# Exchanging the pads of the tile pools: moving blocks of the feed-forward products at 64 instead of 192 bytes mod 256

## The chip, the cores and the metric

The kernel runs on one core of one Trainium2 chip. The metric is the device time of one execution in microseconds (us): 850.94 us before the change, the median of three runs (850.67 to 851.38).

## The reference

Sigmoid attention is followed by two feed-forward stages: a maximum over three products, and then a PReLU stage with a hidden width of 2048. Cut to what matters:

```python
scores = scale * np.matmul(q, k.transpose(0, 1, 3, 2)) - np.log(S)   # 4 x 12 heads, 448 x 64
attn = 1.0 / (1.0 + np.exp(-scores))
x = np.matmul(attn, v)                                               # -> 1792 x 768
h = np.maximum(np.maximum(x @ w1, x @ w2), x @ w3)                   # 768 wide
y = h @ w_out
h = y @ w_in                                                         # 2048 wide
g = np.maximum(h, 0.0) + alpha * np.minimum(h, 0.0)
out = g @ w_out2                                                     # 1792 x 768
```

All arrays are float32.

## The kernel before

**Two parts.** `attention` does scores and the weighted sum of values in 64 by 64 tiles of TensorE, four of them side by side (lines 563 and 584). After it, `ff` and `ff3` do all the feed-forward products. Each product is computed by a scheme with seven block products in place of eight (numbered 0 to 6), and each float32 factor is split into a high and a low float32r part, of which three of the four partial products are kept: low weight by high input, high weight by low input, and high by high. Every partial product is a matmul with a stationary block of 128 x 128 (the weight part) and a moving block of 128 x 448 (the input part); all 3528 of them are issued by `group` at line 694, and each one has its own load of the stationary block. They stand in long runs that add up in one PSUM bank: nine in a run for the products with three blocks of depth (tiles `u_0X`, `u_1W` and so on) and more in the last product (`eX`, `eW`, `eV`).

**What the other engines do meanwhile.** ScalarE and VectorE unpack weights from 64-bit words, form sums and differences of blocks, split them into high and low parts, and move results out of PSUM. A list of pending operations with credits per engine (`op`, `advance`, `need`) decides which of them is put into the program after which product; it counts columns, and addresses do not enter into it.

**Where tiles lie.** Weight tiles (`wslot`, 384 columns of 4 bytes, that is 6 x 256 bytes) come from pools that begin at a multiple of 256 bytes in each partition. Input tiles (`slot`, 448 columns, 7 x 256 bytes) come from pool `a` on the left, and from pools `c` and then `e` on the right, which grow towards lower addresses. A small tile named `pad` is taken once from each pool. In pool `a` it is taken ahead of the slots, so the slots begin that much higher; in the right pools it is taken behind them, and since the pool ends at a fixed address, its slots begin that much lower. In the last product, pool `l` holds weight parts (`lf`) first, then a pad, then the input parts (`rf`). In the built program every one of the 3528 matmuls of line 694 has its stationary block at 0 mod 256 and its moving block at 192 mod 256. In the attention, both operands of every matmul lie at 0 mod 256, before and after the change.

Of the kernel before, what the change touches and what calls it, by code (L numbers as in the profile page):

```python
# [15 lines left out]

P = 128
SCRATCH = 4096
HEADS, BATCH, SEQ, WIDTH, FF2 = 12, 4, 448, 768, 2048
HK = WIDTH // P // 2  # L20
NU, KP = 3 * HK, FF2 // P // 2
# [41 lines left out]
def kernel(  # L63
# [33 lines left out]
    def pad(pool, w):  # L97

        if pool not in padded:
            padded.add(pool)  # L100
            pools[pool].tile([P, w], F32, tag="pad", name=f"pad_{pool}")

    def slot(nm, pool="a", w=TW, dt=F32):
        if pool == "a":
            pad(pool, 48)
        t = pools[pool].tile([P, w], dt, tag="s" + pool, name=nm, bufs=room[pool])
        if pool != "a":
            pad(pool, 16)
        return t

    def wslot(nm, dt=F32, pool="w"):

        if pool != "w":
            return slot(nm, pool, HF, dt)
        return wpool.tile([P, HF], dt, tag="ws", name=nm, bufs=21)
# [91 lines left out]
    def need_ops(*ops):  # L207

        chain = [o for o in ops if o.step is None]
        for o in chain:  # L210
            chain += [d for d in o.deps if d.step is None and d not in chain]
        while any(o.step is None for o in ops):
            now[0] += 1
            n = len(urgent) + len(flow)
            for todo in (urgent, flow):
                for o in [o for o in todo if o in chain]:
                    if ready(o, False) and (o.gate is None or o.gate()):
                        emit(o)
                        todo.remove(o)
            if len(urgent) + len(flow) == n:  # L220
                advance(0, free=True)
            assert now[0] < 99999
# [4 lines left out]
    def drain():  # L227
        while urgent or flow:
            n = len(urgent) + len(flow)
            advance(0, free=True)  # L230
            assert len(urgent) + len(flow) < n or now[0] < 9999
# [182 lines left out]
    def forms(q, of, into, homes, soon=False):  # L414
# [10 lines left out]
        def cut(c, x, *deps):  # L425
            def make(y):
                if y == "h":
                    home[c] = homes(c, 2)
                    take(home[c], 2)
                    if into is hf:  # L430
                        hhome[g, c, r] = home[c]
                return slot(f"{q}_{c}{y}", home[c], TW, F32R)

            o = split_ops(
                into[g, c, r], make, lambda: b[x][0], TW, *deps, gate=lambda: homes(c, 2), soon=soon
            )
            if (c, x) not in ((2, "T"), (1, "21")):
                o.after.append(lambda: used(x))
            return o

        def t1():
            p = homes(None, 1)
            take(p)
            b["T"] = slot(f"{q}_t", p), p
            tensor_op(b["T"][0], b["12"][0], b["11"][0], ALU.subtract)
            used("11")
# [610 lines left out]
    def ff3(ps_m, dpool, fd, wd, slopes, seq, turn_left):  # L1057
# [6 lines left out]
        def tile_l(tag, nm, w, bufs, dt=F32):  # L1064
            return pools["l"].tile([P, w], dt, tag=tag, name=nm, bufs=bufs)
# [144 lines left out]
        def plan():  # L1210
            for n in range(1, 14):
                if n % 2 == 0:
                    for kp in range(KP):
                        left_ops(n // 2, kp)
                for kp in range(KP):
                    right_ops(n, kp)
# [86 lines left out]
        def run(stored):  # L1303
            plan()
            for k in range(7):
                for g, mp in order:
                    if (k, g, mp) == (0, 0, 1):
                        need_ops(*stored, *firsts)
                        turn_left()

                        lf[1, 0]["h"] = tile_l("lf", "lf1_0h", HF, 2 * KP, F32R)
                        pad("l", 48)
                        for x in (2, 3):
                            kept[x, order[0]] = tile_l(f"p{x}", f"p{x}_00", TW, 2 * HK)
                    e_group(k, g, mp)
            drain()
# [3 lines left out]
    with tc.manual_schedule():  # L1320
# [22 lines left out]
        def turn_left():  # L1343
            left.close()
            pools["l"] = ctx.enter_context(
                tc.tile_pool(name="slots_l", bufs=1, reuse_waits="tile")
            )
            del pools["a"]
# [64 lines left out]
```

## Time and profile before

| | before |
|---|---|
| median of 3 runs | 850.94 us (850.67 to 851.38) |
| the profiled execution's own time | 851.17 us |
| its span, first to last instruction | 849.3 us |
| TensorE matmuls busy (PE) | 844.4 us, 99% |
| TensorE weight loads busy (PEld) | 732.8 us, 86% |
| VectorE (DVE) | 655.4 us, 77% |
| ScalarE (ACT) | 517.7 us, 61% |
| GpSimd (POOL) | 146.9 us, 17% |

Busy time is the time in which at least one instruction of the engine ran. Matmuls overlap: the end of one lies past the start of the next, so how fast TensorE goes is read from the time between starts, or from the length of a run in the chain, and not from the duration of one matmul.

### The profile page before, as it was taken

How to read it: one execution, taken by the hardware profiler on the slowest of the kernel's cores; microseconds unless marked ns; L12 is line 12 of the kernel's file. 1: busy time of each engine (PE TensorE's matmuls, PEld its weight loads, DVE VectorE, ACT ScalarE, POOL GpSimd, SP SyncE). 2: the span in 40 equal slices, each digit the busy share in tenths (PEclk: the TensorE clock that was granted, in tenths of full speed). 3: DMA queues.
4: the chain of work that ended last, by engine and by line, in shares of the span. 5: the costliest groups of instructions: out<-in, count | busy, mean ns of one | idle time of the engine just before them, and what ended most of it. 6: DMA issues, size and time to landing. Idle time of an engine off the chain costs nothing.

```text
span 849.3 us, 14230 instructions
## 1 busy us (share of the span) xinstructions
PE 844.4 (99%) x4878; PEld 732.8 (86%) x4878; DVE 655.4 (77%) x1304; ACT 517.7 (61%) x1006; POOL 146.9 (17%) x272
## 2 busy tenths in 40 slices
PE   9999999999999999999999999999999999999998
PEld 4444678999999999999999999999999999999997
DVE  1889888789979988797488988977768687868631
ACT  6888997644655464656377867776657554453530
POOL 1464000003200312410001322221211010001110
PEclk9999999999999999999999999999999999999999
DMA  7899632445845765987531766534547999437111
GB/s 269 277 371 350 214 110 87 131 135 191 284 155 159 240 207 171 360 314 222 157 95 65 243 196 232 184 131 155 172 162 265 328 351 371 144 118 242 69 44 54
DMA packets 77863, 170.45 MB, mean 201 GB/s; under 512 B 11120, under 2 KB 51856, under 8 KB 77792
## 3 DMA queue, kind: packets, MB, share of 16 engines
q1 hardware_dynamic: 60048, 106.38, 39.7%
q0 software_dynamic: 17456, 62.83, 19.6%
q8 instruction: 38, 0.62, 0.3%
q10 hardware_dynamic: 288, 0.34, 0.1%
q14 instruction: 33, 0.27, 0.1%
HBM read 123.12 MB, written 46.40 MB: 200 GB/s over the span
## 4 chain that ended last, share of the span: by engine, by line
PE 99%; DVE 0%; ACT 0%; issue 0%
PE u_0X L694 17%; PE u_1X L694 17%; PE eW L694 10%; PE eX L694 10%; PE u_1W L694 9%; PE u_0W L694 9%; PE sc L563 8%; PE pav L584 7%; PE u_0V L694 4%; PE u_1V L694 4%; PE eV L694 3%; PE warm L629 0%; DVE o L1232 0%; ACT o L1230 0%; DVE zeros L625 0%
## 5 line engine op out<-in xcount | busy, mean ns | idle before, releaser
L571 ACT ACTIVATE a<-sc,bias_s 128x896 f32<-128x896 f32 x84 | 83.2, 1010 | 12.7 <-PE sc L563 11.6
L563 PE MATMUL sc<-qt,kt 64*64 64x448 f32 x672 | 83.1, 540 | 0.0
L584 PE MATMUL pav<-a,vt 64*64 64x448 f32 x672 | 82.0, 536 | 0.0
L281 DVE CUSTOM_DVE_ANT_0 wt<-wr,wt 128x768 uint16<-128x768 uint16 x112 | 62.6, 559 | 3.9
L273 DVE SCALAR_TENSOR_TENSOR wr<-wr 128x384 uint32<-128x384 uint32 x112 | 62.0, 554 | 0.4
L265 ACT ACTIVATE wr<-wr 128x384 uint32<-128x384 uint32 x112 | 62.1, 554 | 0.0
L563 PEld LDWEIGHTS sc<-qt,kt 64*64 64x64 f32 x672 | 36.3, 134 | 29.3 <-issue 14.8
L584 PEld LDWEIGHTS pav<-a,vt 64*64 64x64 f32 x672 | 35.9, 133 | 28.1 <-issue 19.1
L262 ACT ACTIVATE wt<-wr 128x384 f32<-128x384 f32 x92 | 51.0, 554 | 14.7 <-DMA wr<-in_weights_dram 11.6
L741 DVE SCALAR_TENSOR_TENSOR r<-n,nalpha,r 128x448 f32<-128x448 f32 x64 | 42.8, 682 | 14.5 <-ACT n L738 14.4
L774 POOL DMA_DIRECT2D gd<-r x48 | 25.9, 541 | 159.6 <-DVE r L741 145.2
L245 POOL DMA_DIRECT2D wd<-wt x32 | 17.7, 553 | 174.4 <-DVE wt L281 173.6
L889 ACT COPY u<-u_1X 128x448 f32<-128x448 f32 x40 | 21.3, 533 | 38.5 <-PE u_1X L694 38.4
L272 DVE TENSOR_SCALAR wt<-wt 128x384 uint32<-128x384 uint32 x112 | 39.8, 355 | 5.5 <-ACT wt L262 4.8
L889 ACT COPY u<-u_0X 128x448 f32<-128x448 f32 x40 | 21.3, 533 | 35.6 <-PE u_0X L694 35.5
L874 ACT COPY u_0V<-u_0X 128x448 f32<-128x448 f32 x20 | 10.3, 518 | 48.0 <-PE u_0X L694 48.0
L311 DVE TENSOR_TENSOR u<-u_1W,u 128x448 f32<-128x448 f32 x34 | 21.2, 623 | 23.8 <-ACT u L889 19.5
L311 DVE TENSOR_TENSOR u<-u_0W,u 128x448 f32<-128x448 f32 x34 | 21.2, 623 | 18.3 <-ACT u L889 14.4
L1287 ACT COPY p<-eW 128x448 f32<-128x448 f32 x12 | 6.4, 534 | 34.1 <-PE eW L694 34.1
L599 DVE COPY x<-pav 128x448 f32<-128x448 f32 x12 | 7.5, 624 | 22.3 <-PE pav L584 22.3
L737 ACT ACTIVATE r<-u 128x448 f32<-128x448 f32 x32 | 18.5, 579 | 5.6 <-DVE u L311 5.6
L311 DVE TENSOR_TENSOR p<-eX,p 128x448 f32<-128x448 f32 x12 | 7.5, 623 | 16.4 <-PE eX L694 16.4
(821 smaller groups left out, 2791.7 us busy)
## 6 DMA issues: line engine op xcount, KB each, us to landing
wr<-in_weights_dram SPq DMA_DIRECT2D x100, 384.0 KB, 3.6
gl<-gd SPq DMA_DIRECT2D x79, 224.0 KB, 4.4
wl<-wd SPq DMA_DIRECT2D x64, 192.0 KB, 4.5
gd<-r POOLq DMA_DIRECT2D x48, 224.0 KB, 2.7
gl_T<-gdT SPq DMA_DIRECT2D x32, 224.0 KB, 5.1
hr<-hd POOLq DMA_DIRECT2D x28, 224.0 KB, 5.9
wd<-wt POOLq DMA_DIRECT2D x32, 192.0 KB, 3.8
kt<-in_k_dram SPq DMA_DIRECT2D x23, 224.0 KB, 5.3
```

The source lines that it names most:

```text
L262: nc.scalar.activation(st["T"].bitcast(F32), st["r"][:, :, 1].bitcast(F32), AF.Abs, scale=2.0**-112)
L265: nc.scalar.activation(st["r"][:, :, 0], st["r"][:, :, 0], AF.Copy, scale=2.0**-29)
L272: nc.vector.tensor_scalar(st["T"], st["T"], 3, None, ALU.logical_shift_left)
L273: nc.vector.scalar_tensor_tensor(out=st["r"][:, :, 0], in0=st["r"][:, :, 1], scalar=0x80000000, in1=st["r"][:, :, 0], op0=ALU.bitwise_and, ...
L281: nc.vector.tensor_tensor(out=st["T"], in0=st["r"][:, :, 0], in1=st["T"], op=ALU.add)
L311: nc.vector.tensor_tensor(out=out, in0=a, in1=b, op=op)
L563: nc.tensor.matmul(sc[g * KH : (g + 1) * KH, j, :S], keys[u, z][r, m * KH : (m + 1) * KH], queries[u, z][r], start=True, stop=True,)
L571: nc.scalar.activation(a, sc[:, :, :S], AF.Sigmoid, bias=bias_s, scale=scale)
L584: nc.tensor.matmul(pv[key][j * D : (j + 1) * D, :S], vts[u][r, m, j], a[r, j], start=start, stop=stop,)
L694: nc.tensor.matmul(ps[:, : rh.shape[-1]], lt, rh, start=(start and z == 0), stop=(stop and z == len(mms) - 1), skip_group_check=True,)
L741: nc.vector.scalar_tensor_tensor(out=s["r"], in0=s["n"], scalar=nalpha[:, f : f + 1], in1=s["r"], op0=ALU.mult, op1=ALU.add,)
L889: nc.scalar.copy(side[u, g, k], banks[X][:, :TW])
```

## The change

The two pad sizes change places: 16 columns (64 bytes) stand ahead of the slots in pools `a` and `l` where there were 48 (192 bytes), and 48 columns behind those in the right pools where there were 16.

```diff
+PAD = 16
...
     def slot(nm, pool="a", w=TW, dt=F32):
         if pool == "a":
-            pad(pool, 48)
+            pad(pool, PAD)
         t = pools[pool].tile([P, w], dt, tag="s" + pool, name=nm, bufs=room[pool])
         if pool != "a":
-            pad(pool, 16)
+            pad(pool, 64 - PAD)
         return t
...
                         lf[1, 0]["h"] = tile_l("lf", "lf1_0h", HF, 2 * KP, F32R)
-                        pad("l", 48)
+                        pad("l", PAD)
```

In the built program the moving block of all 3528 matmuls of line 694 begins at 64 mod 256 instead of 192; their stationary blocks stay at 0. The same tiles are also read and written by ScalarE, VectorE and DMAs, at 64 instead of 192. No instruction and no wait is added, removed or put elsewhere on any engine or queue: each engine's sequence, waits included, is the same but for the numbers of source lines.

## Rows read from the trace of the kernel before

**Rows 1.** The page, busy time (us, share of the span) and instructions of each engine.

```profile
PE 844.4 (99%) x4878; PEld 732.8 (86%) x4878; DVE 655.4 (77%) x1304; ACT 517.7 (61%) x1006; POOL 146.9 (17%) x272
```

**Rows 2.** Cores: span and mean granted TensorE clock.

```profile
core 0: 849.3 us, clock 0.999
```

**Rows 3.** The page, the chain that ended last, by engine and by line.

```profile
PE 99%; DVE 0%; ACT 0%; issue 0%
PE u_0X L694 17%; PE u_1X L694 17%; PE eW L694 10%; PE eX L694 10%; PE u_1W L694 9%; PE u_0W L694 9%; PE sc L563 8%; PE pav L584 7%; PE u_0V L694 4%; PE u_1V L694 4%; PE eV L694 3%; PE warm L629 0%; DVE o L1232 0%; ACT o L1230 0%; DVE zeros L625 0%
```

**Rows 4.** Waits of PE: who for whom, us in total, times, longest.

```profile
PE warm L629 <- DVE zeros L625: 1.2, 1, 1.2
```

**Rows 5.** Windows: attention, feed-forward products, tail; each engine's busy us (instructions), clock, DMA.

```profile
core 0: us, PE busy (x) PEld busy (x) DVE busy (x) ACT busy (x) POOL busy (x), PEclk, DMA share, GB/s
3.97:131.98 128.01, 128.01 (x1345) 70.79 (x1345) 100.42 (x220) 111.47 (x149) 35.69 (x65) 1.00 0.75 264
131.98:845.60 713.62, 713.62 (x3529) 661.21 (x3528) 554.24 (x1081) 404.44 (x854) 108.30 (x199) 1.00 0.57 190
845.60:849.30 3.70, 0.02 (x1) 0.00 (x0) 0.39 (x1) 0.35 (x1) 0.00 (x0) 0.84 0.19 62
```

**Rows 6.** The chain in order of time, feed-forward: start us, us, what.

```profile
201.34 1.82 PE u_0X L694 x9
203.16 1.82 PE u_1X L694 x9
```

**Rows 7.** Timeline of PE and PEld in the feed-forward: start us, us, what.

```profile
193.29 0.37 PE L694 MATMUL u_1W<-x_2h,f_2l 128*128 128x448 f32 x1
193.30 0.19 PEld L694 LDWEIGHTS u_1W<-x_2l,f_2h 128*128 128x128 f32 x1
193.50 0.36 PE L694 MATMUL u_1W<-x_2l,f_2h 128*128 128x448 f32 x1
193.50 0.19 PEld L694 LDWEIGHTS u_1W<-x_2h,f_2h 128*128 128x128 f32 x1
193.70 0.36 PE L694 MATMUL u_1W<-x_2h,f_2h 128*128 128x448 f32 x1
193.70 0.19 PEld L694 LDWEIGHTS u_0X<-x_3h,f_3l 128*128 128x128 f32 x1
193.90 0.37 PE L694 MATMUL u_0X<-x_3h,f_3l 128*128 128x448 f32 x1
```

**Rows 8.** Line 694: duration ns min/median/max, first and last start us, form.

```profile
L694 PEld LDWEIGHTS u_0W<-x_2h,f_2l x27: 187/187/188, 133.6 to 340.5; 128*128 128x128 f32 x27
L694 PE MATMUL u_0W<-x_2h,f_2l x27: 363/367/368, 133.8 to 340.7; 128*128 128x448 f32 x27
L694 PE MATMUL u_0W<-x_2l,f_2h x27: 361/361/368, 134.0 to 340.9; 128*128 128x448 f32 x27
L694 PE MATMUL u_0W<-x_2h,f_2h x27: 361/363/363, 134.7 to 341.1; 128*128 128x448 f32 x27
```

**Rows 9.** Line 563, weight loads of the attention, columns as in rows 8.

```profile
L563 PEld LDWEIGHTS sc<-qt,kt x672: 129/133/228, 3.9 to 128.8; 64*64 64x64 f32 x168
```

**Rows 10.** The chain in order of time, attention, columns as in rows 6.

```profile
59.74 0.75 PE sc L563 x8
60.49 0.75 PE pav L584 x8
...
66.50 0.75 PE pav L584 x8
67.26 0.74 PE sc L563 x7
```

**Rows 11.** Groups by line: busy us, mean ns of one, idle us before it and releaser.

```profile
L311 DVE TENSOR_TENSOR wt<-wt,wt 128x384 f32<-128x384 f32 x36 | 19.8, 551 | 0.2
L311 DVE TENSOR_TENSOR gl_T<-gl,gl_T 128x448 f32<-128x448 f32 x32 | 18.2, 620 | 0.0
```

**Rows 12.** The page, DMA issues: count, KB each, median us to landing.

```profile
gl<-gd SPq DMA_DIRECT2D x79, 224.0 KB, 4.4
wl<-wd SPq DMA_DIRECT2D x64, 192.0 KB, 4.5
```

## Prediction

> **What bounds the kernel now.** I read the busy time of the engines first: matmuls cover 99% of the span [rows 1], at a granted clock of 0.999, that is the 2.4 GHz level [rows 2]. Next the chain that ended last: it is PE for 99%, nearly all of that line 694 [rows 3]. Then PE's waits: a single one, 1.2 us, before the first matmul of all [rows 4]. So nothing that another engine or a DMA does holds TensorE up; the time is the number of matmuls times the time from one to the next. By stage, the attention takes 128.0 us, the feed-forward products 713.6 us and the tail 3.7 us [rows 5]. The profiled execution took 851.17 us with a span of 849.3, so 1.9 us lie around the span; it stands 0.23 us above the median of 850.94. The sum below is made against 851.17.
>
> The change touches the 713.6 us alone. There the window holds 3529 matmuls (one of them the attention's last), so 713.62 / 3529 = 202.2 ns from one to the next, and the chain says the same: nine in 1.82 us [rows 5, 6]. It is the same in every run of nine, whichever tiles are used.
>
> What fills these 202.2 ns? A block has 448 columns; at one column a tick of 2.4 GHz they need 186.7 ns (an estimate). The attention gives a check. From 59.74 to 67.26 us it does 80 matmuls in 7.52 us, 376 ns for the four that run side by side, against 2 x 186.7 = 373.3 ns for two passes over the columns: 2.7 ns over the stream [rows 10]. A feed-forward matmul takes 202.2, some 15 ns over its stream. The weight load explains most of that. The timeline shows each load starting within 0.01 us of the matmul ahead of it, and the next matmul starting some 0.20 us after that [rows 7]. The load lasts 187 to 188 ns [rows 8]. So load, hand-over, matmul start, next load is a closed chain, about 187.5 plus 15 ns, and the stream of the moving block is inside it, with about 202.2 - 186.7 - 2.7 = 13 ns to spare.
>
> The steps are not equal. Starts in the timeline are 0.20 or 0.21 us apart [rows 7], and the three matmuls of a triple have median durations of 367, 361 and 363 ns [rows 8]. The reader is to see a pattern of three with about 6.5 ns between the long and the short ones. With two short steps and a long one in 606.6 ns, the short one is (606.6 - 6.5) / 3 = 200.0 ns and the long one 206.5 ns. Something costs 6.5 ns in one step of three, and it is not a wait for another engine. A read of the moving block that meets the load in the same part of the memory would do that; no row proves it.
>
> **The change part by part.** It removes, adds and moves no instruction, so each term is a number of accesses at a new place times what that place adds.
>
> The attention: 0 ns, as its operands stay where they are.
>
> VectorE, ScalarE and DMAs on blocks that move from 192 to 64: taken as nothing. A VectorE sum of 384 columns at 0 mod 256 takes 551 ns, one of 448 columns at 192 takes 620 [rows 11], 1.43 and 1.38 ns a column, so no cost of the place shows. A transfer of 224 KB into blocks at 192 lands in 4.4 us, one of 192 KB into blocks at 0 in 4.5 [rows 12]. The cover is large: VectorE is busy 554 of 713.6 us and ScalarE 404 [rows 5], and PE waits for neither. Even 5% more on VectorE, 28 us, would fit in the 159 us that it is free, as long as it is spread out.
>
> The 3528 matmuls: here everything is decided, one ns on each is 3.5 us. The trace of before has only one place of the moving block against the stationary one in these products (192 against 0), so the cost is bounded from both sides. The nearest bounds are the two kinds of step that are there already. If every step is the short one, (200.0 - 202.2) x 3528 = -7.7 us, 843.4. If every step is the long one, (206.5 - 202.2) x 3528 = +15.3 us, 866.4. The far bound below is the stream alone, 186.7 + 2.7 = 189.4 ns, -45 us or 806; I leave it out of the range, since it needs a load that is no longer in the chain, and the loads last 187 ns wherever one looks. Above there is no such far row.
>
> Which value? The two streams can be followed by an estimate. The moving block's 1792 bytes pass in 186.7 ns, 9.6 bytes a ns. A load of 64 columns takes 133 ns [rows 9], one of 128 takes 187.5, so 64 columns cost 54 ns, a column 0.85 ns, and the weights are read at 4.7 bytes a ns for 108 ns. Both begin together [rows 7]. If the memory repeats every 256 bytes, which I assume and no row shows, a block at 192 is 64 bytes behind the weights' 0 and gains 4.9 bytes a ns: it meets the load at 13 ns and at 65 ns, and would meet it a third time at 118, when the load is over. A block at 64 is 192 behind and meets it at 39 and 91 ns. Two meetings either way; but the second now falls in the last 17 ns of the load. A load delayed there passes all of it on to the next matmul, while after a meeting at 13 ns the two are still settling. So I take the long step as the more frequent one after the change: two of three, (200.0 + 2 x 206.5) / 3 = 204.3 ns, +2.15 x 3528 = +7.6 us. The sum: 851.17 + 0 + 0 + 7.6 = 858.8 us.
>
> The Trainium skill speaks against any effect: TensorE: Matmul & The Clock Gate, in "Step-by-step: what each phase is for", says that TensorE reads SBUF through two independent ports, one for the moving operand and one for weights, so that loading the next weights takes no bandwidth from a running matmul. By it the third term is 0 and the sum 851.2. The even 187 to 188 ns of the loads agree with it; the pattern of three steps is not explained by it.
>
> **The rivals.**
>
> The place makes no difference (no change). Two meetings before and two after may cost the same; or the memory repeats every 128 bytes or less, and then 64 and 192, which are 128 apart, are the same place. For it: loads are equally long in 3528 cases [rows 8], and a rate of 0.85 ns a column fits the attention's loads, where both operands are at 0, and those of the feed-forward with 192 against 0 [rows 8, 9]; and the moving stream has 13 ns to spare, which hides a delay of its own. Against it: the step of 206.5 ns that comes and goes without any wait. Time: 851.2, from 850 to 852.
>
> The long step goes away (faster). If what costs 6.5 ns is the early meeting at 13 ns, when load and matmul have both just begun, a block at 64 has none before 39 ns, and all steps are short: 851.17 - 7.7 = 843.4. For it: the short step is what two of three matmuls take already. It decides from half a ns per matmul (1.7 us). Against it: with the other meeting still at 91 ns, there is no reason that the step stays short. VectorE is not in the way, 554 us of work in then 706.
>
> Every step becomes long: 866.4, the far end of the forecast's own case. For it: an even meeting in each load. Against it: the pattern of three shows that the delay shifts the next meeting.
>
> That the change does not do what it says is excluded, since the built program has all 3528 blocks at 64.
>
> **How the numbers follow.** Slower, 0.42: mostly 853 to 867, a tenth of the case beyond. No change, 0.30: 850 to 852. Faster, 0.28: from 849 down to 842 in most of it, and by less likely ways further down. The forecast is that of the likeliest, 858.8. Its own range is 853 to 867. From 842 to 867 lie about 0.36 + 0.30 + 0.20 = 0.86; I keep these ends, since both bounds of the unknown cost are inside them by little. About 0.2% (1.7 us) is what a measurement of this kernel can tell from no change; with it the chances are 0.28 faster, 0.30 same, 0.42 slower.
>
> **What the profile after would show.** If I am right, runs of nine in the chain take 1.84 us and not 1.82, the window of the products grows to about 721 us with PE still at 100% of it and no wait of PE, the attention stays at 128.0 us, and the medians of the three kinds of matmul show 367 twice. With all steps long, nine take 1.86 us; with all short, 1.80; if the place is without effect, 1.82 and the same three medians. Loads that last longer than 188 ns would show that it is the load that is delayed; loads of 187 with longer steps, that it is the hand-over or the stream. The prediction is wrong if the long step becomes rarer or disappears, if the meeting of two reads costs nothing, or if a wait of PE for VectorE appears, which would mean that the other engines feel the place after all.

## The result, and the profile after

The changed kernel takes 843.57 us (median of 6 runs, 842.73 to 844.59), the kernel before 850.99 us in the same comparison: a ratio of 0.991 with a 95% interval of 0.9897 to 0.9923. It is 7.4 us faster. Medians, ratios and intervals leave out executions over 1.5% above a kernel's shortest; in this document these are three of the ten of the kernel with both kinds of block at 0 (866.43 to 867.58 us, at a granted clock of 0.999 to 1.0 as in the other seven, and without a trace). The forecast was 858.8 us and slower; what came is, to 0.2 us, the number of the second rival (843.4, "the long step goes away").

The page of the kernel after: the span, and below it busy time, share and instructions of each engine, to be held against [rows 1].

```profile
span 840.9 us, 14230 instructions
PE 835.9 (99%) x4878; PEld 724.5 (86%) x4878; DVE 654.8 (78%) x1304; ACT 517.2 (62%) x1006; POOL 146.8 (17%) x272
```

Against [rows 1] PE lost 8.5 us of busy time; VectorE and ScalarE lost 0.6 and 0.5. PE still waits once only:

```profile
PE warm L630 <- DVE zeros L626: 1.2, 1, 1.2
```

The windows of the kernel after by stage, the products from their start at 131.31 us to their end at 837.15 [rows 5]:

```profile
core 0: us, PE busy (x) PEld busy (x) DVE busy (x) ACT busy (x) POOL busy (x), PEclk, DMA share, GB/s
3.96:131.31 127.35, 127.35 (x1346) 62.56 (x1345) 100.39 (x220) 111.46 (x149) 35.66 (x65) 1.00 0.76 266
131.31:837.15 705.84, 705.83 (x3529) 661.18 (x3528) 553.68 (x1081) 403.87 (x854) 108.30 (x199) 1.00 0.58 192
```

The products went from 713.6 to 705.8 us, 7.8 us less over 3529 matmuls, 2.2 ns on each. The span fell by 8.4 us; the other 0.66 us is an attention of 127.35 and not 128.01 us. Its blocks did not move, and in the kernels measured below the products start from 0.6 us earlier to 1.2 us later than before (counted from the first matmul) without regard to the places, so I count this as scatter.

The chain in order of time, as in [rows 6], shows the gain in each run of nine: 1.80 and not 1.82 us.

```profile
199.92 1.80 PE u_0X L695 x9
201.72 1.80 PE u_1X L695 x9
203.52 1.80 PE u_0W L695 x9
```

Line 695 (694 before), duration ns min/median/max, to be read beside [rows 8]: the loads last as long as before, and where the three medians were 367, 361 and 363 they are now 360, 362 and 363, without a long one.

```profile
L695 PEld LDWEIGHTS u_0W<-x_2h,f_2l x27: 187/187/188, 133.0 to 337.6; 128*128 128x128 f32 x27
L695 PE MATMUL u_0W<-x_2h,f_2l x27: 360/360/363, 133.2 to 337.8; 128*128 128x448 f32 x27
L695 PE MATMUL u_0W<-x_2l,f_2h x27: 360/362/363, 133.4 to 338.0; 128*128 128x448 f32 x27
L695 PE MATMUL u_0W<-x_2h,f_2h x27: 362/363/363, 134.0 to 338.2; 128*128 128x448 f32 x27
```

The start times in the trace give the step itself, the time from one matmul of this line to the next. Its mean is the time from the first to the last start, divided by 3527: 713.34 us / 3527 = 202.25 ns before, 705.53 / 3527 = 200.04 ns after. Before, the steps repeat 199, 201, 207; after, 198, 201, 201.

VectorE and the transfers, as in [rows 11, 12], did not notice the new place:

```profile
L312 DVE TENSOR_TENSOR wt<-wt,wt 128x384 f32<-128x384 f32 x36 | 19.8, 550 | 0.2
L312 DVE TENSOR_TENSOR gl_T<-gl,gl_T 128x448 f32<-128x448 f32 x32 | 18.2, 616 | 0.0
...
gl<-gd SPq DMA_DIRECT2D x79, 224.0 KB, 4.3
wl<-wd SPq DMA_DIRECT2D x64, 192.0 KB, 4.5
```

### The profile page after: what moved, and what is told of

It reads as the page before. It is cut to its first block, busy times and chain, and to the rows that moved or that the text cites. A ratio compares the mean times of both kernels' runs of the same rounds, so it can differ in the third digit from the quotient of the medians.

```text
span 840.9 us, 14230 instructions
## 1 busy us (share of the span) xinstructions
PE 835.9 (99%) x4878; PEld 724.5 (86%) x4878; DVE 654.8 (78%) x1304; ACT 517.2 (62%) x1006; POOL 146.8 (17%) x272
## 4 chain that ended last, share of the span: by engine, by line
PE 99%; DVE 0%; ACT 0%; issue 0%
PE u_0X L695 17%; PE u_1X L695 17%; PE eW L695 10%; PE eX L695 10%; PE u_0W L695 9%; PE u_1W L695 9%; PE sc L564 8%; PE pav L585 8%; PE u_0V L695 4%; PE u_1V L695 4%; PE eV L695 3%; PE warm L630 0%; DVE o L1233 0%; ACT o L1231 0%; DVE zeros L626 0%
## 5 line engine op out<-in xcount | busy, mean ns | idle before, releaser
L564 PE MATMUL sc<-qt,kt 64*64 64x448 f32 x672 | 79.4, 540 | 0.0
L585 PE MATMUL pav<-a,vt 64*64 64x448 f32 x672 | 78.7, 536 | 0.0
L263 ACT ACTIVATE wt<-wr 128x384 f32<-128x384 f32 x92 | 50.8, 553 | 14.9 <-DMA wr<-in_weights_dram 11.7
L564 PEld LDWEIGHTS sc<-qt,kt 64*64 64x64 f32 x672 | 31.5, 134 | 32.7 <-issue 19.9
L585 PEld LDWEIGHTS pav<-a,vt 64*64 64x64 f32 x672 | 31.1, 133 | 32.2 <-issue 27.9
L312 DVE TENSOR_TENSOR wt<-wt,wt 128x384 f32<-128x384 f32 x36 | 19.8, 550 | 0.2
```

The lines of the kernel that those rows point to most:

```text
L263: nc.scalar.activation(st["T"].bitcast(F32), st["r"][:, :, 1].bitcast(F32), AF.Abs, scale=2.0**-112)
L312: nc.vector.tensor_tensor(out=out, in0=a, in1=b, op=op)
L564: nc.tensor.matmul(sc[g * KH : (g + 1) * KH, j, :S], keys[u, z][r, m * KH : (m + 1) * KH], queries[u, z][r], start=True, stop=True,)
L585: nc.tensor.matmul(pv[key][j * D : (j + 1) * D, :S], vts[u][r, m, j], a[r, j], start=start, stop=stop,)
```

## The experiments

The theories: the difference between the places of the moving and the stationary block decides (DIFFERENCE), or the moving block's own place (OWN PLACE), or other engines (OTHERS); and, for what a step is made of, a chain of loads (CHAIN), stops where the two streams meet (MEETING), or a fixed cost when the weights change (HAND-OVER). In the diffs, STAT and MOVE are the places of the stationary and the moving blocks mod 256, lines left out are marked by three dots, and the lines taken out are those of the changed kernel. A mean step is the time from the first to the last start of a kernel's 3528 products, divided by 3527, unless the text says otherwise. "The kernel before" measured beside the runs was at 851.2 to 851.8 us.

### Only the difference of the places counts

Both kinds of block moved, with a wider tile ahead of the weights' pool:

```diff
+STAT, MOVE = 128, 64
...
-            pad(pool, PAD)
+            pad(pool, (MOVE - STAT) % 256 // 4)
...
-            pad(pool, 64 - PAD)
+            pad(pool, -MOVE % 256 // 4)
...
-    bias_s = const.tile([P, 32], F32, name="bias_s")[:, :1]
+    bias_s = const.tile([P, 32 + STAT // 4], F32, name="bias_s")[:, :1]
...
-                        pad("l", PAD)
+                        pad("l", (MOVE - STAT) % 256 // 4)
```

Stationary at 128, moving at 64:

> Stationary blocks at 128 and moving blocks at 64 mod 256, so the moving block lies 192 ahead of the stationary one as in the kernel before, while it begins where it does in the changed kernel. If only the difference of the two places counts (theory DIFFERENCE, the picture of two streams that meet): steps of 199, 201 and 207 ns, mean 202.2, and about 851 us. If the moving block's own place counts (rival OWN PLACE): mean step 200.0 and about 843.5 us. If the gain came from VectorE, ScalarE or DMAs at the new place (rival OTHERS): 843.5 us as well, since their blocks stay at 64.

Measured: 850.96 us, ratio 0.9995 (0.9986 to 1.0005), mean step 202.25 ns. The gain is gone though the moving blocks, which VectorE, ScalarE and the DMAs use too, lie where they do in the changed kernel. PE waits once only, 1.2 us, here as there. OWN PLACE and OTHERS fall. The chain of this kernel:

```profile
299.85 1.82 PE u_0X L695 x9
301.67 1.82 PE u_1X L695 x9
```

The mirror image, stationary at 128 and moving at 192 (`STAT, MOVE = 128, 192`):

> Moving blocks at 192 as in the kernel before, stationary ones at 128, so the moving block lies 64 ahead of the stationary one as in the changed kernel. DIFFERENCE: steps of 198 and 201 ns, mean 200.0, and 843.5 us, though the moving block begins where it did before and VectorE, ScalarE and DMAs find their blocks at 192. Any theory by which 64 itself is the better place: 851 us.

Measured: 843.73 us, ratio 0.9905 (0.9888 to 0.9921), mean step 200.03 ns. The moving blocks lie where they did before the change, and the whole gain is there. Its chain:

```profile
300.17 1.80 PE u_1X L695 x9
301.96 1.80 PE u_0X L695 x9
```

So DIFFERENCE holds for these two: 64 ahead is the fast pair and 192 ahead the slow one, at both places of the stationary blocks that were tried. Since 64 minus 128 does the same as 192 minus 0, and 64 and 192 differ, the pattern repeats after 256 bytes and not after 128.

### Each matmul pays for its own moving block

One part of the change alone, the left pools at 64 and the right ones at 192:

```diff
         if pool != "a":
-            pad(pool, 64 - PAD)
+            pad(pool, 16)
```

> One part of the change alone: moving blocks in the left pools at 64, in the right pools at 192, as before. In the last product, whole runs read from one side: the right-hand runs (first half of the tokens) should keep mean steps of 202.2 ns, the left-hand runs should have 200.0 (PAIR: the place of the block that is being read, against the stationary ones, counts for its own step). SPILL: the place of one run changes the steps of the next, so that both halves have steps between.

Measured: 847.58 us in one run, between the two kernels, mean step 201.04 ns. In the last product the halves alternate. The chain inside one stretch that reads the right pools and one that reads the left ones:

```profile
639.21 12.94 PE eX L695 x64
...
652.96 13.21 PE eX L695 x66
```

12.94 / 64 = 202.2 ns and 13.21 / 66 = 200.2 ns, within one kernel and 14 us of each other. SPILL falls: the step follows the moving block that is being read. All stationary blocks lie at 0 here, so the run does not tell whether the stationary block that counts is the matmul's own or the next one's, which is loaded meanwhile.

### Other differences

`STAT, MOVE = 0, 128` and `0, 0`:

> Moving blocks at 128, stationary at 0. DIFFERENCE with a repeat every 256 bytes: the two streams meet at 26, 78 us/1000 (ns) of the load; a step different from both 200.0 and 202.2 is possible, between 197.5 and 207 ns, 835 to 867 us. If the memory repeated every 128 bytes, 64 and 192 would have been equal, which the result excludes. OWN PLACE gives no number here.

> Moving and stationary blocks both at 0, no pads. DIFFERENCE: the streams meet at the start, in the middle and at the very end of the load, three times and not twice, so the step should be longer than in either kernel: over 202.2 ns, over 851 us. OWN PLACE: no number, but 0 is the place that begins a line of 256, so it would be the best or equal: 843 us or less.

Measured: 857.32 us, ratio 1.0072 (1.0057 to 1.0088), mean step 204.03 ns with 128; 852.95 us (median of the seven counted, 851.87 to 854.08), ratio 1.0019 (1.0008 to 1.003), mean step 202.70 ns with 0. Both are slower than the kernel before. A run of nine in the chain with 128:

```profile
300.72 1.84 PE u_0X L695 x9
```

OWN PLACE, by which 0 is the best or equal, falls once more. 0 is a little over 202.2 ns, as three meetings would have it, but 128, which by my picture is met twice like 64 and 192, is the worst of the four. The picture of counted meetings does not rank them.

`STAT, MOVE = 0, 96` and `0, 32`, off the multiples of 64:

> Moving blocks at 96, half way between 64 (step 200.0) and 128 (204.0), stationary at 0. MEETING: the mean step lies between, 200 to 204 ns, 843 to 858 us; if places count only by whole 64 bytes it equals one of the two.

> Moving blocks at 32, half way between 0 (step 202.7) and 64 (200.0); at 96 the step was 205.4, above both its neighbours 64 (200.0) and 128 (204.0). LINE: a block that does not begin on a multiple of 64 bytes touches 29 and not 28 pieces of 64 bytes, and each piece takes 6.67 ns or a part of it: 204 ns or more here too, over 856 us. SMOOTH: between 200.0 and 202.7, 843 to 853 us.

Measured in one run each: 862.49 us and 205.36 ns with 96, 866.77 us and 206.70 ns with 32. Both are slower than either neighbour, so SMOOTH falls, and with 96 both expectations do (200 to 204 ns, or the step of a neighbour). With 32 every step has the same length, 206 or 207 ns, 6.66 over the mean with 64; by an estimate 16 columns, or 64 bytes, at one column a tick of 2.4 GHz take 6.67. That is what LINE expects for a 29th piece, but 96 pays 5.3 ns, so LINE does not give that step by itself. Stationary blocks stayed at 0 in both runs, so it is open whether the moving block's own place or the difference makes these two slow. The loads are no longer for it: with 32, the longest steps of these places, 3526 of the 3528 loads last 188 ns. The chain of the kernel with 32:

```profile
301.34 1.86 PE u_1X L695 x9
303.20 1.86 PE u_0X L695 x9
```

### The load does not set the step

A narrower moving block in all matmuls of a run but its first, which leaves terms out of the other columns:

```diff
+            w = rh.shape[-1] if start and z == 0 else 384
             nc.tensor.matmul(
-                ps[:, : rh.shape[-1]], lt, rh, start=(start and z == 0), ...
+                ps[:, :w], lt, rh[:, :w], start=(start and z == 0), ...
```

> As the changed kernel, but all matmuls of a run save its first use 384 of the 448 moving columns, so 64 columns of the outputs miss most of their terms. If the load chain sets the step (CHAIN, the prediction's reading): the step of the narrow matmuls stays near 200 ns, since the loads are the same, and the time stays at 843 us within 1%. If the moving stream sets it (STREAM): 384 columns need 160 ns, the step falls to 160 to 175 ns, and TensorE begins to wait for VectorE, whose 554 us of work fits in no less than that: 730 to 780 us.

Measured: 776.93 us, ratio 0.9132 (0.911 to 0.9154), mean step of the narrow matmuls 173.3 ns, waits left out. A long stretch of the chain, 24.98 / 144 = 173.5 ns, and two loads of this kernel, 0.19 us long and 0.17 us apart:

```profile
744.91 24.98 PE eW L696 x144
...
300.26 0.19 PEld L696 LDWEIGHTS u_0W<-x_2h,f_2l 128*128 128x128 f32 x1
300.43 0.19 PEld L696 LDWEIGHTS u_0W<-x_2l,f_2h 128*128 128x128 f32 x1
```

CHAIN falls, and with it the prediction's reading of the step. The same with 256 columns:

> As the changed kernel, but all matmuls of a run save its first use 256 of the 448 moving columns, so the other columns of the outputs miss most of their terms. STREAM PLUS 13.3 (the step is the moving stream and a fixed hand-over): 106.7 + 13.3 = 120.0 ns. LOAD BINDS AT LAST: a load of 128 columns needs about 108 ns of reading and lasts 187 in the trace; where it sets the step, the step stays between 121 and 202 ns. TensorE may wait for VectorE here, so that the time itself says nothing.

Measured: mean narrow step 117 ns at a granted clock of 1.00, waits left out (732.56 us in one run; TensorE now waits for ScalarE and VectorE). The timeline of PE and PEld in such a stretch shows a load of 0.19 us starting every 0.12 us:

```profile
300.92 0.28 PE L696 MATMUL u_0X<-x_4l,f_4h 128*128 128x256 f32 x1
300.92 0.19 PEld L696 LDWEIGHTS u_0X<-x_4h,f_4l 128*128 128x128 f32 x1
301.04 0.28 PE L696 MATMUL u_0X<-x_4h,f_4l 128*128 128x256 f32 x1
301.04 0.19 PEld L696 LDWEIGHTS u_0X<-x_4l,f_4h 128*128 128x128 f32 x1
```

The next load begins before this one ends, and so does the matmul that uses it. The 187 ns of a load are thus not a time in which the next one has to wait: loads can follow each other at 117 ns. LOAD BINDS AT LAST falls, and STREAM PLUS 13.3 is 3 ns too high. The step is the moving stream (186.7, 160, 106.7 ns, estimates at one column a tick of 2.4 GHz) plus 13.3, 13.3 and 10.7 ns.

This kernel also shows the same matmuls at the lower level of the clock. At 303.11 us a matmul starts after a wait of 1.09 us for ScalarE; in the stretch that follows it the granted clock is 0.50, the 1.2 GHz level:

```profile
core 0: us, PE busy (x) PEld busy (x) DVE busy (x) ACT busy (x) POOL busy (x), PEclk, DMA share, GB/s
303.70:308.90 5.20, 5.20 (x26) 5.20 (x26) 5.10 (x11) 2.12 (x6) 0.54 (x1) 0.50 0.71 217
```

Here and in the other such stretches the steps are 213 or 214 ns, mean 213.3, which is 256 columns at one a tick of 1.2 GHz (213.3) with nothing on top, though each matmul changes its weights as before. In the kernel with 384 columns the steps at a granted clock of 0.50 are 320 ns, again 384 columns at one a tick. The 10.7 ns are there only at the upper level of the clock, so they are not a fixed time that every change of weights costs; HAND-OVER in that form falls. And with 384 columns at the place of before (`STAT, MOVE = 0, 192`):

> As the kernel before (moving blocks at 192), but with 384 of the 448 columns in all matmuls of a run save its first, so 64 columns of the outputs miss most of their terms. With 64 the step was 173.3 ns. If the place costs the same part of a step at any length of the stream: 173.3 + 2.2 = 175.5. If the extra comes from where the stream stands when the load ends, which a shorter stream shifts: another extra, from 0 to 4 ns.

Measured: mean narrow step 174.9 ns, 1.6 more than at 64, where the full stream pays 2.2; 780.68 us in one run. The place costs at either length. The first expectation (175.5) is missed by 0.6 ns; the second, another extra from 0 to 4 ns, holds, but is so wide that little could have failed it.

### What the 13.3 ns and the extra are not

A load of half the columns, which leaves terms out of half of the rows:

```diff
+            h = P if start and z == 0 else P // 2
             nc.tensor.matmul(
-                ps[:, : rh.shape[-1]], lt, rh, start=(start and z == 0), ...
+                ps[:h, : rh.shape[-1]], lt[:, :h], rh, start=(start and z == 0), ...
```

> As the changed kernel, but each matmul of a run save its first loads only 64 of its 128 stationary columns, so half of the output rows miss most of their terms. The moving stream keeps its 448 columns. The runs so far left two theories of the 13.3 ns by which a step exceeds its stream (200.0 - 186.7, and 173.3 - 160 with 384 columns). MEETING: each time the stream passes the load in the memory it stops for 6.67 ns, twice per load of 128 columns when the blocks lie at 64 and 0; a load of 64 columns is over in half the time and is met once: step 193.3 ns. HAND-OVER: a fixed 13.3 ns to change the weights: step 200.0 ns as before.

Measured: mean step 201.52 ns, 849.74 us in one run. Half the load does not save half of the 13.3 ns, so these are not two stops per load: MEETING falls as an account of them. HAND-OVER's 200.0 comes near, but there are 1.5 ns more, with steps from 195 to 209 ns: a shorter load changes the pattern too.

The moving block read in another order, so that both streams go through the memory at one rate:

```diff
             nc.tensor.matmul(
-                ps[:, : rh.shape[-1]], lt, rh, start=(start and z == 0), ...
+                ps[:, : rh.shape[-1]].rearrange("p (b c u) -> p c b u", b=2, u=4), lt,
+                rh.rearrange("p (b c u) -> p c b u", b=2, u=4), start=(start and z == 0), ...
```

> The changed kernel, all sums as they were, but a matmul reads its moving block in another order: four columns of the first half, four of the second half, and so on, and writes each to its own place in PSUM. The halves lie 896 bytes apart, 128 mod 256, and each is read at the rate at which the load reads the weights, so the two streams keep their distance: at 64 and 192 from the load's place all the time. MEETING: they never meet, the step falls to the stream's 186.7 ns plus at most 2.7, and the time to 806 us, or a little more where TensorE then waits for VectorE. HAND-OVER: step 200.0, 843.5 us. A third theory, STRIDE: jumps every 16 bytes make the stream itself slower, 950 us and more.

> The same order of reading with the moving block at 0: its halves lie at 0 and 128 from the load's place. MEETING: one half is in the load's place all the time that the load lasts (108 ns), so the step is longer than any seen so far, over 204 ns. HAND-OVER: between 200.0 and 204 ns. STRIDE: as in the kernel with 64, 950 us and more.

Measured: 890.74 us, ratio 1.0463 (1.0445 to 1.048), and 890.53 us, ratio 1.0458 (1.0442 to 1.0473), mean step 213.36 ns in both. The jumps make the stream slower, though by less than STRIDE had it; whether those in reading or those in writing to PSUM, which come along, is not shown. The place no longer changes the mean, but it changes the single steps: with 64 they alternate between 210 and 216 or 217 ns, with 0 all are 213 or 214. Since the rate of the stream changed together with the distance, these runs say nothing for or against the other two theories.

A stationary block of every second column, so products of other weights:

```diff
-        tuple(left[x][:, r * P : (r + 1) * P] for x in range(2)),
+        tuple(left[x][:, (0, 1, P)[r] : (0, 1, P)[r] + 2 * P - 1 : 2] for x in range(2)),
...
-    a, b = three(tuple(l[x][:, mp * P : (mp + 1) * P] for x in range(2)), ...
+    s = (0, 1, P)[mp]
+    a, b = three(tuple(l[x][:, s : s + 2 * P - 1 : 2] for x in range(2)), ...
```

> The changed kernel with a stationary block of every second column of 255 instead of 128 neighbours, so the products are of other weights; nothing else is changed. The load now moves through the memory at 8 bytes where it moved at 4, as fast as the stream, and keeps its distance of 64 from it. MEETING, what is left of it (a part of a step's cost is that stream and load come to the same quarter of 256 bytes): at 64 there was no extra before, none now, 200.0 ns; if the 13.3 ns are two meetings after all, 186.7 to 189.4. START (only where both begin counts): 200.0.

> The same stationary blocks of every second column with the moving block at 128, whose step was 204.0 ns with neighbouring columns. MEETING: the two streams stay 128 apart for the whole load and never meet, so the extra of 4 ns goes: 200.0 ns. START: the extra stays, 204.0 ns.

In both kernels one stationary block in three starts with the second column, at 4 and not 0 mod 256, so that the distance is 60 (or 124) for it; that part is not separated.

Measured: with 64, mean step 203.37 ns and 854.77 us; with 128, 203.51 ns and 855.79 us, one run each. With 64 neither theory's 200.0 comes. With 128 the mean hides two stretches, which the chain shows:

```profile
251.18 1.80 PE u_0X L695 x9
252.98 1.80 PE u_1X L695 x9
...
400.06 1.85 PE u_1W L695 x9
403.75 1.84 PE u_1V L695 x9
```

The first 1080 matmuls go at 200.0 ns each. At 348.2 us one step takes 223 ns; the load in it waits for a semaphore and starts 0.10 us after the matmul ahead of it. From there on the steps repeat 203, 206, 205, 206, later 207, 202, 206, 205, with a mean of 205.0 until the end. Blocks at the same places thus have two rates in one execution. That the two streams, moving at one rate, keep the offset in time that the disturbance left them would fit an interplay of the two reads; it is argued, not shown, and at 64 the pattern changes at the same matmul (from 205, 201, 205, 202 to 200, 207) with the mean at 203.3 to 203.4 on both sides.

## Why the prediction was wrong

**What bounds the kernel** was right: the products alone changed, PE waits for nobody, and 3528 matmuls at 2.2 ns each make 7.8 of the 8.4 us of the span.

**The reading of the step** as a closed chain of load, hand-over, matmul start and next load was wrong. The kernels with 384 and 256 columns run at 173 and 117 ns with loads that still last 187 to 188 ns at the upper level of the clock. The stream of the moving block is what sets the step, with 13.3 ns on top at the best place, and there is no 13 ns to spare that would hide a delay of the stream. That a load lasts about as long as the stream of 448 columns is a coincidence, which I took for a cause. I also gave rows 8 as showing 3528 equal loads, where they show 27; in the whole trace they last 186 to 189 ns.

**The bounds** held: "if every step is the short one", 843.4 us, is where the kernel went, with the steps' mean at 200.04 ns. The steps are not the short ones of before, though (199 and 201 then, now 198, 201, 201), so that the two means agree to 0.1 ns is in part luck.

**The step that failed is the choice of value, "two of three" steps long.** It rested on the second meeting falling in the last 17 ns of the load, from where a delay would go on to the next matmul. What the runs showed in its place: no step is long, the three repeat 198, 201, 201, and each matmul lost 2.2 ns (202.25 to 200.04) where 2.15 were to be added. The parts of the argument do not hold either. A load does not hold the next matmul in this way: with 256 columns a matmul starts 0.12 us after its load has begun and before that load ends. And the picture of two streams that meet at computed times neither ranks the four places (128 is the worst, 64 the best) nor accounts for a load of half the columns or for one at the stream's rate. The sign was chosen on a picture for which no row stood; the rows gave a bound on either side and nothing to choose between them.

**The terms of nothing** for VectorE, ScalarE and DMAs were right, and the two kernels with stationary blocks at 128 show it: the blocks that these engines share with TensorE lie at 64 without the gain, and at 192 with it.

**The rivals.** "The place makes no difference" is excluded. The Trainium skill's two independent ports (TensorE: Matmul & The Clock Gate, "Step-by-step: what each phase is for") do not describe this: moving only the stationary blocks by 128 bytes changes the step by 2.2 ns in either direction, so the step depends on both places together, and the measurement decides. "Every step becomes long" did not come. "The long step goes away" gave the time; its cause, an early meeting at 13 ns, was not shown, and stands no better than my own.

**What is shown and what is open.** Shown: the cost of a place is paid by each matmul for its own moving block, and is 0 at 64, 2.2 ns at 192, 2.7 at 0 and 4.0 at 128 (moving minus stationary, mod 256, over 200.04 ns). That only the difference counts was tested for 64 and 192; 0 and 128 were measured with stationary blocks at 0 alone. Not shown is by which conflict of the two reads these numbers come about, nor why what a step has over its stream is gone at the lower level of the clock. That the mean steps with 64, 192, 0 and 128 lie 0, 1/3, 2/5 and 3/5 of 6.67 ns above the lowest is an observation that a theory would have to give; mine does not. That a stop happens in such units was not tried by itself.

## What to carry to other kernels

Where TensorE is busy throughout and waits for nothing, compare the step between matmuls with the time of the moving stream: here 202.2 against 186.7 ns, and part of the difference, 2.2 ns or 1% of the products, was a matter of addresses alone. Try the place of moving blocks against stationary ones, mod 256 and in steps of 64 bytes, by measurement; the four places differ by 1.6% of the time here, and the two places off a multiple of 64 bytes that were tried, 32 and 96, were worse than any of them (one run each). Do not take the duration of a weight load for the time until the next one can start: shorten the stream and see whether the step follows.

## What the runs showed of the hardware that was not expected

- A weight load of 128 float32r columns lasts 187 ns in the trace, yet a new one started every 117 ns with 256 moving columns (granted clock 1.00).
- At a granted clock of 0.50, 256 moving columns take 213.3 ns a step, 1 column a tick of 1.2 GHz with nothing on top; at 1.00 they take 117, 10.7 over the stream.
- Over the stream of the moving block, a step has 13.3 ns more with 448 and with 384 columns at the best place, and half the stationary columns do not lower it (14.9 ns with 64 of 128).
- Moving blocks at 32 mod 256 take 206.7 ns in every step, 6.7 more than the mean with 64.
- Reading the moving block in pieces of 16 bytes from two halves, and writing the results in the same order, raises the mean step to 213.4 ns, at two places alike.
- With every second stationary column and moving blocks at 128, the mean step went from 200.0 to 205.0 ns at one disturbed step of 223 ns and stayed there.
